# Weights first, batch 0's small loads on another queue: a fused sparse-attention and FFN kernel on one core

## The chip, the cores and the metric

The kernel runs on one core of one Trainium2 chip. The metric is device time in microseconds (us). One core has five engines that run their own instruction streams: TensorE (PE in the profile; its weight loads are PEld), VectorE (DVE), ScalarE (ACT), GpSimd (POOL) and SyncE (SP). Loads and stores are done by 16 DMA engines; SP and ACT issue them, each on a queue of its own (q1 and q10 in the profile).

## The reference

Eight batches of attention with 8 heads, 576 tokens and 64 values a head. Heads 0 to 3 look back over 32 tokens, heads 4 to 7 at the earlier tokens of the same place modulo 32. The 4608 x 512 result goes through a feed-forward layer without activation.

```python
mask_local = (rel >= 0) & (rel < stride)                       # stride = 32
mask_strided = (rel >= 0) & (pos[None, :] % stride == pos[:, None] % stride)
scores = np.where(masks[None], scale * q @ k^T, -1e9)          # local: heads 0-3, strided: heads 4-7
attn = softmax(scores)
x = (attn @ v).transpose(0, 2, 1, 3).reshape(B * S, H * D)     # 4608 x 512
a = x @ w1                                                     # w1, w2: 512 x 1024
b = x @ w2
h = a * b @ w3                                                 # w3: 1024 x 1024
out = h @ w_out                                                # w_out: 1024 x 512
```

Inputs and output are f32 in HBM.

## The kernel before

**The fold.** Since nothing stands between `w3` and `w_out`, the kernel first computes their product `w34` (1024 x 512, f16). For each of 8 row blocks `jc` of `w3`, `fold_tr(jc)` transposes the block on PE (8 transposes, line 357) into PSUM, and DVE and ACT each copy one half to `w3T` (lines 359 and 360). `fold_mm(jc)` gives two halves of 4 matmuls of 512 columns each (line 335): `h0` uses the part of `w3T` that DVE copied, `h1` the part that ACT copied; after `h1` the block of `w34` is cast by DVE or ACT in turn. Every half needs `w_out`, all of it by the end of `fold_mm(0)`. The 23 units of the fold stand in the order h0(0), tr(1), h1(0), h0(1), tr(2), h1(1) and so on.

**Attention** works on pairs of heads; pairs 0 and 1 of a batch are local, 2 and 3 strided. A pair's steps: `ph_T` transposes q and k on PE (line 214), copies by ACT or DVE; `ph_R` does the same for the last 64 tokens (line 230), once a batch; `ph_S` computes scores (line 248), ACT the exponential (line 253), DVE the mask (line 255); `ph_PV` multiplies by v (line 268) and DVE divides by the sum (lines 274, 276); `ph_T2` transposes back (line 284) and ACT copies into `xT` (line 70 or 291). Batch 0 has 21 such steps.

**The feed-forward layer** runs over 9 tiles of 512 tokens: `ab_halves` computes a and b (lines 312, 321; 16 units) and their product on DVE (line 323), `o_halves` the output (line 335, 8 units), which ACT copies and stores (lines 346, 347).

**Order.** PE's instructions are pinned in program order. `host` writes that order out: it runs through the units of the fold or of a tile and puts steps of the attention between them, from the unit after `lead` on, spread evenly over the rest, so that after the last unit the stream has come to a given step. Before the change batch 0's 21 steps are spread over the last 20 of the fold's 23 units (`lead=3`), and 8 steps of batch 1 over the last 7 of the 16 `ab` units of tile 0 (`lead=9`). The other engines' orders are found by a scheduler at build time, from the program order and a model of when data is there. Each engine then works in order.

**Loads.** All loads are issued by SP, in program order, into `stgp`, a ring of 9 staging buffers of 4 KB a partition; a load waits until the cast of the ninth load before it is done. Casts to f16 go mostly to POOL (line 74; `load_w12` gives `w1` to ACT, line 70). Row sizes in HBM, as the loads take them: `w3` 4 KB (`load_w3`, line 141), `w_out` 2 KB (`load_wo`, line 136), q and k 1 KB (`load_qk`, line 159), `w1`, `w2` 1 KB (`load_w12`, line 150), the last 64 tokens of q and k 256 B, 512 rows each (`load_rest`, line 168), v of the local heads 256 B, 4 transfers of 576 rows (`load_vL`, line 179), v of the strided heads 2 KB (`load_vS`, lines 190 and 191). The cast blocks of `w3` have 4 buffers (`w3n`), so the cast of block jc + 4 waits for `fold_tr(jc)`.

Before the change `w3`'s eight blocks are loaded in between batch 0's loads, as the end of the listing shows.

Of the kernel before, what the change touches and what calls it, by code (L numbers as in the profile page):

```python
# [8 lines left out]
FP32 = mybir.dt.float32  # L9
# [10 lines left out]
def kernel(  # L20
# [11 lines left out]
    nc = tc.nc  # L32
    B, H, S, D = q.shape
# [3 lines left out]
    P = 128  # L37
# [10 lines left out]
    LQ, LT = 96, 6  # L48
    SQ, ST = 72, 8
    NM = 512  # L50
# [4 lines left out]
    stgp = ctx.enter_context(tc.tile_pool(name="stgp", bufs=9))  # L55
# [9 lines left out]
    def pe(ins):  # L65
        return tc.keep_in_program_order(ins)

    def copy(eng, out, in_):
        if eng == "a":
            nc.scalar.copy(out=out, in_=in_)  # L70
        elif eng == "v":
            nc.vector.tensor_copy(out=out, in_=in_)  # L72
        else:
            nc.gpsimd.tensor_copy(out=out, in_=in_)  # L74
# [46 lines left out]
    xT = [consts.tile([P, NTOK], FP16, name=f"xT{cc}") for cc in range(4)]  # L121
# [11 lines left out]
    def load_wo(g, eng):  # L133
        src = moe_w_out.rearrange("(c p) n -> p c n", p=P)
        st = stgp.tile([P, 2, DM], FP32, tag="stg")
        nc.sync.dma_start(st, src[:, 2 * g:2 * g + 2, :])
        copy(eng, woh[:, 2 * g:2 * g + 2, :], st)

    def load_w3(jc, eng):
        st = stgp.tile([P, DF], FP32, tag="stg")  # L140
        nc.sync.dma_start(st, moe_w3[bass.ds(jc * P, P), :])
        t = ffn.tile([P, DF], FP16, tag="w3n", bufs=4)
        w3n[jc] = t
        copy(eng, t, st)

    def load_w12(g):
        cs = bass.ds(g * 256, 256)
        for wd, wh, eng in ((moe_w1, w1h, "a"), (moe_w2, w2h, "p")):
            st = stgp.tile([P, KM, 256], FP32, tag="stg")
            nc.sync.dma_start(st, wd.rearrange("(c p) n -> p c n", p=P)[:, :, cs])  # L150
            copy(eng, wh[:, :, cs], st)


    x16 = {}

    def load_qk(b, grp, engs="pp"):
        for nm, ten, eng in (("q", q, engs[0]), ("k", k, engs[1])):
            st = stgp.tile([P, 4, 4, D], FP32, tag="stg")
            nc.sync.dma_start(st.rearrange("p h c d -> p h (c d)"),
                              ten[b, 4 * grp:4 * grp + 4, 0:NM].rearrange("h (p c) d -> p h (c d)", c=4))  # L160
            t = qkp.tile([P, 4, 4, D], FP16, tag=f"{nm}{grp}")
            copy(eng, t, st.rearrange("p h c d -> p c h d"))
            x16[(b, nm, grp)] = t

    def load_rest(b, eng="p"):
        st = stgp.tile([P, H, D], FP32, tag="stg")
        for i, ten in enumerate((q, k)):
            nc.sync.dma_start(st[64 * i:64 * i + 64], ten[b, :, NM:S].rearrange("h p d -> p h d"))
        t = qkp.tile([P, H, D], FP16, tag="r")
        copy(eng, t, st)  # L170
        x16[(b, "r")] = t

    def load_vL(b):
        vt = v16L[b % 2]
        for hp in range(2):
            hs = slice(2 * hp, 2 * hp + 2)
            st = stgp.tile([P, 2, LT, D], FP32, tag="stg")
            for h in range(2):
                nc.sync.dma_start(st[32:P, h], v[b, 2 * hp + h].rearrange("(t p) d -> p t d", p=LQ))
            for pr in (bass.ds(32, 32), bass.ds(64, 64)):  # L180
                nc.gpsimd.tensor_copy(out=vt[pr, hs, :, 0:D], in_=st[pr])  # L181
            nc.vector.tensor_copy(out=vt[0:32, hs, 1:LT, 0:D], in_=vt[96:P, hs, 0:LT - 1, 0:D])

    def load_vS(b):
        vt = v16S[b % 2]
        for hp in range(2):
            st = stgp.tile([SQ, 2, ST, D], FP32, tag="stg")
            sf = st.rearrange("p h c d -> p h (c d)")
            sv = v[b, 4 + 2 * hp:6 + 2 * hp].rearrange("h (p c) d -> p h (c d)", c=ST)
            nc.sync.dma_start(sf[0:64], sv[0:64])  # L190
            nc.sync.dma_start(sf[64:SQ], sv[64:SQ])
            nc.gpsimd.tensor_copy(out=vt[:, 2 * hp:2 * hp + 2, :, 0:D], in_=st)  # L192


# [102 lines left out]
    def ab_halves(tch):  # L297
        tok = bass.ds(tch * NT, NT)
        res = []

        def first():
            abts[tch] = ffn.tile([P, KF, NT], FP16, tag="abt", bufs=4, name=f"abt{tch}")

        for jc in range(KF):
            st = {}

            def a(jc=jc, st=st):
                if jc == 0:
                    first()
                aps = psF.tile([P, NT], FP32, tag="f")  # L310
                for ci in range(KM):
                    pe(nc.tensor.matmul(aps, w1h[:, ci, bass.ds(jc * P, P)], xT[ci][:, tok],  # L312
                                        start=(ci == 0), stop=(ci == KM - 1)))
                asb = ffn.tile([P, NT], FP32, tag="asb")
                nc.scalar.copy(out=asb, in_=aps)  # L315
                st["asb"] = asb

            def bb(jc=jc, st=st):
                bps = psF.tile([P, NT], FP32, tag="f")
                for ci in range(KM):  # L320
                    pe(nc.tensor.matmul(bps, w2h[:, ci, bass.ds(jc * P, P)], xT[ci][:, tok],  # L321
                                        start=(ci == 0), stop=(ci == KM - 1)))
                nc.vector.tensor_mul(abts[tch][:, jc, :], bps, st["asb"])  # L323

            res += [a, bb]
        return res
# [26 lines left out]
    def fold_tr(jc):  # L353
        js = bass.ds(jc * P, P)
        ps = psF.tile([P, 1024], FP16, tag="f", name="trp")
        for kc in range(KF):
            pe(nc.tensor.transpose(ps[:, kc * P:(kc + 1) * P], w3n[jc][:, bass.ds(kc * P, P)], id16))
        pv = ps.rearrange("x (c j) -> x c j", j=P)
        nc.vector.tensor_copy(out=w3T[0][:, :, js], in_=pv[:, 0:4, :])
        nc.scalar.copy(out=w3T[1][:, :, js], in_=pv[:, 4:8, :])  # L360

    def fold_mm(jc):
        js = bass.ds(jc * P, P)

        def done(ps):
            copy("va"[jc % 2], w34[:, jc, :], ps)

        return acc_halves(lambda kc: w3T[kc // 4][:, kc % 4, js], lambda kc: woh[:, kc, :], done)
# [3 lines left out]
    batch_end = {}  # L372
# [4 lines left out]
    for b in range(B):  # L377
# [4 lines left out]
        for i in range(4):  # L382
            p = 4 * b + i
# [14 lines left out]
    pos = [0]  # L398

    def host(units, upto, lead=0):  # L400
        n = len(units) - lead
        p0 = pos[0]
        for i, u in enumerate(units):
            u()
            tgt = p0 + ((upto - p0) * max(i + 1 - lead, 0)) // n
            while pos[0] < tgt:
                stream[pos[0]]()
                pos[0] += 1


    load_w3(0, "p")
    for g in range(4):
        load_wo(g, "p")
    load_w3(1, "p")
    load_qk(0, 0)
    load_rest(0)
    load_w3(2, "p")
    load_vL(0)
    load_w3(3, "p")
    load_qk(0, 1)  # L420
    load_w3(4, "p")
    load_w3(5, "p")
    load_vS(0)
    load_w3(6, "p")
    load_w3(7, "p")
    load_w12(0)
    load_w12(1)
    load_w12(2)
    load_qk(1, 0)
    load_rest(1)  # L430
    load_w12(3)
    load_vL(1)
    load_qk(1, 1)
    load_vS(1)

    fold = []
    fold_tr(0)
    for jc in range(KF):
        h0, h1 = fold_mm(jc)
        fold.append(h0)  # L440
        if jc + 1 < KF:
            fold.append(lambda jc=jc: fold_tr(jc + 1))
        fold.append(h1)
    host(fold, batch_end[0], lead=3)
    load_qk(2, 0)
    load_rest(2)
    load_vL(2)
    host(ab_halves(0), pos[0] + 8, lead=9)
    load_qk(2, 1)
    load_vS(2)  # L450
    host(o_halves(0), batch_end[1])
    for tch in range(1, NTILE):
# [46 lines left out]
```

## Time and profile before

| what | value |
|---|---|
| median of 3 runs | 295.0 us (292.44 to 295.15) |
| profiled execution | span 299.8 us, 6132 instructions |
| PE busy | 268.9 us, 90% of the span |
| DVE busy | 174.6 us, 58% |
| ACT busy | 147.1 us, 49% |
| POOL busy | 102.1 us, 34% |
| bytes moved | 48.64 MB, mean 162 GB/s |

The profiled execution's time is its span; recording it makes it longer than the runs without a profile. Busy shares are averages over the whole span: the first 50 us hold the fold and batch 0, the middle a mix of attention and feed-forward tiles, and from about 200 us on the last tiles have less attention beside them. A group's releaser is what ended the idle time before it, and only the idle time of the engine that bounds a stretch costs anything.

### The profile page before, as it was taken

To read this page: it belongs to the slowest core of one execution; us is meant where nothing else is said; L and a number is where in the kernel's file an instruction comes from. 1 tells how busy PE (TensorE), PEld (TensorE's weight loads), DVE (VectorE), ACT (ScalarE), POOL (GpSimd) and SP (SyncE) were. 2 spreads that over 40 slices of the span, in tenths; PEclk is the share of its full clock that TensorE was granted. 3 is DMA by queue.
4 is the path that set the end of the run, shared out by engine and by line. 5 is a ranking of instruction groups with operands and counts; after the bars stand their busy time and mean duration, and the time that the engine had idled before them with its cause. 6 is when DMAs were issued, how large, how long until landed. Compare 5 with 4: busy or idle time off the path is not lost.

```text
span 299.8 us, 6132 instructions
## 1 busy us (share of the span) xinstructions
PE 268.9 (90%) x2401; PEld 141.6 (47%) x2401; DVE 174.6 (58%) x353; ACT 147.1 (49%) x269; POOL 102.1 (34%) x118
## 2 busy tenths in 40 slices
PE   2258898989889989989999899999999999999995
PEld 1025554435545545545555445555555555444442
DVE  2011775357888866886789659747765774340430
ACT  2025586557565545536645554564455445333332
POOL 5539744486626724653455345110000000000000
PEclk9996999999999999999999999999999999999999
DMA  7999999999869929994896796030012002003003
GB/s 228 349 160 352 288 348 258 216 273 209 249 200 243 242 79 270 246 178 159 240 236 140 253 193 164 27 115 2 2 57 87 0 2 105 35 2 116 24 2 140
DMA packets 58653, 48.64 MB, mean 162 GB/s; under 512 B 29184, under 2 KB 49664, under 8 KB 58624
## 3 DMA queue, kind: packets, MB, share of 16 engines
q1 hardware_dynamic: 53440, 38.81, 54.7%
q10 hardware_dynamic: 5184, 9.44, 8.7%
q8 instruction: 19, 0.31, 0.5%
q14 instruction: 10, 0.08, 0.1%
HBM read 38.80 MB, written 9.44 MB: 161 GB/s over the span
## 4 chain that ended last, share of the span: by engine, by line
PE 67%; DVE 9%; DMA 9%; ACT 9%; issue 3%; SPq 1%; POOL 0%; ACTq 0%
PE ops L335 19%; PE bps L321 18%; PE aps L312 16%; PE xps L268 4%; PE ps L214 4%; DMA st<-in_moe_w_dram 4%; ACT pte L253 3%; DVE ptm L255 3%; DMA st<-in_moe_w_out_dram 3%; DMA out_dram<-osb 3%; PE sps L248 2%; PE ps L284 2%; DVE abt L323 2%; ACT xT L291 2%; DVE kT L72 2%
## 5 line engine op out<-in xcount | busy, mean ns | idle before, releaser
L312 PE MATMUL aps<-xT,w1h 128*128 128x512 f16 x288 | 75.3, 379 | 3.2 <-ACT xT L291 3.0
L323 DVE TENSOR_TENSOR abt<-bps,asb 128x512 f16<-128x512 f32 x72 | 49.5, 687 | 47.2 <-PE bps L321 45.5
L321 PE MATMUL bps<-xT,w2h 128*128 128x512 f16 x288 | 74.0, 379 | 0.0
L315 ACT COPY asb<-aps 128x512 f32<-128x512 f32 x72 | 42.2, 586 | 64.6 <-PE aps L312 61.8
L335 PE MATMUL ops<-w,abt 128*128 128x512 f16 x288 | 71.7, 379 | 0.5 <-DVE abt L323 0.5
L74 POOL CAST t<-st 128x1024 f16<-128x1024 f32 (+1 forms) x48 | 47.4, 991 | 43.4 <-DMA st<-in_k_dram 29.1
L253 ACT ACTIVATE pte<-sps 128x576 f16<-128x576 f32 (+1 forms) x64 | 38.4, 650 | 7.3 <-PE sps L248 7.1
L276 DVE TENSOR_TENSOR xqs<-xps,rcp 96x384 f16<-96x384 f32 (+1 forms) x64 | 39.6, 619 | 2.0
L321 PEld LDWEIGHTS <-w2h 128*128 128x128 f16 x288 | 25.8, 97 | 31.6 <-issue 5.1
L70 ACT COPY qT<-ps 128x512 f16<-128x512 f16 (+1 forms) x48 | 22.9, 481 | 29.9 <-PE ps L214 23.8
L346 ACT COPY osb<-ops 128x512 f32<-128x512 f32 x36 | 21.1, 586 | 29.9 <-PE ops L335 28.6
L335 PEld LDWEIGHTS <-abt 128*128 128x128 f16 x288 | 24.7, 98 | 23.1 <-DVE abt L323 1.0
L312 PEld LDWEIGHTS <-w1h 128*128 128x128 f16 x288 | 25.1, 98 | 22.2
L181 POOL CAST v16L<-st 32x768 f16<-32x768 f32 (+1 forms) x32 | 27.1, 847 | 18.4 <-DMA st<-in_v_dram 12.6
L268 PEld LDWEIGHTS <-ptm 72*128 72x128 f16 (+1 forms) x448 | 21.4, 97 | 19.2 <-DVE ptm L255 6.4
L255 DVE TENSOR_TENSOR ptm<-pte,maskL 128x576 f16<-128x576 f16 x32 | 20.5, 646 | 11.7 <-ACT pte L253 11.2
L72 DVE COPY kT<-ps 128x512 f16<-128x512 f16 (+1 forms) x36 | 18.8, 535 | 10.1 <-ACT qT L70 10.0
L255 DVE TENSOR_TENSOR ptm<-pte,maskS 72x576 f16<-72x576 f16 x32 | 19.6, 620 | 8.5 <-ACT pte L253 7.9
L192 POOL CAST v16S<-st 72x1024 f16<-72x1024 f32 x16 | 16.9, 1055 | 20.1 <-PE xps L268 11.4
L335 PE MATMUL ops<-woh,w3T 128*128 128x512 f16 x64 | 19.8, 440 | 3.2 <-POOL woh L74 3.1
L214 PEld LDWEIGHTS <-t 128*128 128x128 f16 x256 | 17.1, 99 | 8.8 <-issue 2.6
L214 PE MATMUL ps<-id,t 128*128 128x128 f16 x256 | 20.1, 222 | 0.5 <-POOL t L74 0.5
(48 smaller groups left out, 175.8 us busy)
## 6 DMA issues: line engine op xcount, KB each, us to landing
out_dram<-osb ACTq DMA_DIRECT2D x36, 256.0 KB, 2.0
st<-in_moe_w_dram SPq DMA_DIRECT2D x16, 512.0 KB, 8.9
st<-in_q_dram SPq DMA_DIRECT2D x16, 512.0 KB, 5.5
st<-in_k_dram SPq DMA_DIRECT2D x16, 512.0 KB, 6.6
st<-in_v_dram SPq DMA_DIRECT2D x32, 144.0 KB, 6.1
st<-in_v_dram SPq DMA_DIRECT2D x16, 256.0 KB, 7.2
st<-in_moe_w_out_dram SPq DMA_DIRECT2D x4, 512.0 KB, 8.5
st<-in_q_dram SPq DMA_DIRECT2D x8, 128.0 KB, 8.1
```

The source lines that it names most:

```text
L74: nc.gpsimd.tensor_copy(out=out, in_=in_)
L181: nc.gpsimd.tensor_copy(out=vt[pr, hs, :, 0:D], in_=st[pr])
L214: pe(nc.tensor.transpose(ps[:, i, c * P:(c + 1) * P], src[:, c, h0:h0 + 2].rearrange("p h d -> p (h d)"), id16))
L253: nc.scalar.activation(out=pte[0:kr], in_=sps[0:kr, :, 0:288], func=AF.Exp, bias=0.0, scale=scale)
L255: nc.vector.tensor_mul(ptm[0:kr, 0:576].rearrange("p (a x) -> p a x", x=w), pte[0:kr].rearrange("p h (a x) -> p (h a) x", x=w), _ap(mk, 0, ...
L268: pe(nc.tensor.matmul(xps[:, h, i * 65:(i + 1) * 65], ptm[0:kr, c0:c0 + P], vt[0:kr, 2 * (s.hp % 2) + h, g * m + i, :], start=True, stop=T ...
L276: nc.vector.tensor_mul(xqs[0:w, 0:m].rearrange("p i h d -> p h i d"), xv[:, :, :, 0:D], _ap(rcp, 0, [[rp, w], [4, 2], [1, m], [0, D]]))
L312: pe(nc.tensor.matmul(aps, w1h[:, ci, bass.ds(jc * P, P)], xT[ci][:, tok], start=(ci == 0), stop=(ci == KM - 1)))
L315: nc.scalar.copy(out=asb, in_=aps)
L321: pe(nc.tensor.matmul(bps, w2h[:, ci, bass.ds(jc * P, P)], xT[ci][:, tok], start=(ci == 0), stop=(ci == KM - 1)))
L323: nc.vector.tensor_mul(abts[tch][:, jc, :], bps, st["asb"])
L335: pe(nc.tensor.matmul(st["ps"], lhs(ci), rhs(ci), start=(ci == 0), stop=(ci == KF - 1)))
```

## The change

SP now issues `w3(0)`, the four parts of `w_out` and `w3(1)` to `w3(4)` one after the other, then q and k of heads 0 to 3, `w3(5)`, q and k of heads 4 to 7, `w3(6)`, `w3(7)`. Batch 0's `load_rest`, `load_vL` and `load_vS` go to ACT's queue: ten transfers, issued behind ACT's copy of `fold_tr(0)` and pinned there. They don't use the staging ring but columns of `xT` that are written only from batch 2 on. Seven of the casts of `w3` and `w_out` move from POOL to DVE. Batch 0's 21 steps are spread over the last 8 of the fold's 23 units (`lead=15`), and in tile 0 the steps of batch 1 begin two units later (`lead=11`).

```diff
+    def spare(cc, n):
+        return xT[cc][:, 2 * S:2 * S + 2 * n].bitcast(FP32)
+
+    def act_dma(out, in_):
+        pe(nc.scalar.dma_start(out, in_))
...
-    def load_rest(b, eng="p"):
-        st = stgp.tile([P, H, D], FP32, tag="stg")
+    def load_rest(b, early=False):
+        if early:
+            st = spare(3, H * D).rearrange("p (h d) -> p h d", h=H)
+        else:
+            st = stgp.tile([P, H, D], FP32, tag="stg")
+        dma = act_dma if early else nc.sync.dma_start
         for i, ten in enumerate((q, k)):
-            nc.sync.dma_start(st[64 * i:64 * i + 64], ...)
+            dma(st[64 * i:64 * i + 64], ...)
...
-    def load_vL(b):
+    def load_vL(b, early=False):
...
+            if early:
+                st = spare(0, 4 * LT * D).rearrange("p (h t d) -> p h t d", h=4, t=LT)[:, hs]
+            else:
+                st = stgp.tile([P, 2, LT, D], FP32, tag="stg")
+            dma = act_dma if early else nc.sync.dma_start
...
-    def load_vS(b):
+    def load_vS(b, early=False):
...
+            if early:
+                st = spare(1 + hp, 2 * ST * D)[0:SQ].rearrange("p (h c d) -> p h c d", h=2, c=ST)
+            else:
+                st = stgp.tile([SQ, 2, ST, D], FP32, tag="stg")
+            dma = act_dma if early else nc.sync.dma_start
...
-    load_w3(0, "p")
+    load_w3(0, "v")
     for g in range(4):
-        load_wo(g, "p")
-    load_w3(1, "p")
+        load_wo(g, "pv"[g % 2])
+    for jc in range(1, 5):
+        load_w3(jc, "pv"[jc % 2])
     load_qk(0, 0)
-    load_rest(0)
-    load_w3(2, "p")
-    load_vL(0)
-    load_w3(3, "p")
+    load_w3(5, "v")
     load_qk(0, 1)
-    load_w3(4, "p")
-    load_w3(5, "p")
-    load_vS(0)
     load_w3(6, "p")
-    load_w3(7, "p")
+    load_w3(7, "v")
     load_w12(0)
...
     fold_tr(0)
+    load_rest(0, early=True)
+    load_vL(0, early=True)
+    load_vS(0, early=True)
...
-    host(fold, batch_end[0], lead=3)
+    host(fold, batch_end[0], lead=15)
...
-    host(ab_halves(0), pos[0] + 8, lead=9)
+    host(ab_halves(0), pos[0] + 8, lead=11)
```

More of the change, by code (lines that the diff above doesn't have):

```diff
@@ L163, in load_qk @@
             x16[(b, nm, grp)] = t
-    def load_rest(b, eng="p"):
-        st = stgp.tile([P, H, D], FP32, tag="stg")
+    def load_rest(b, early=False):
[4 more added lines that the diff above has]
+        dma = act_dma if early else nc.sync.dma_start
         for i, ten in enumerate((q, k)):
-            nc.sync.dma_start(st[64 * i:64 * i + 64], ten[b, :, NM:S].rearrange("h p d -> p h d"))
+            dma(st[64 * i:64 * i + 64], ten[b, :, NM:S].rearrange("h p d -> p h d"))
         t = qkp.tile([P, H, D], FP16, tag="r")
-        copy(eng, t, st)
+        copy("p", t, st)
         x16[(b, "r")] = t
-    def load_vL(b):
+    def load_vL(b, early=False):
         vt = v16L[b % 2]
@@ L176, in load_vL @@
             hs = slice(2 * hp, 2 * hp + 2)
-            st = stgp.tile([P, 2, LT, D], FP32, tag="stg")
+            if early:
[3 more added lines that the diff above has]
+            dma = act_dma if early else nc.sync.dma_start
             for h in range(2):
-                nc.sync.dma_start(st[32:P, h], v[b, 2 * hp + h].rearrange("(t p) d -> p t d", p=LQ))
+                dma(st[32:P, h], v[b, 2 * hp + h].rearrange("(t p) d -> p t d", p=LQ))
             for pr in (bass.ds(32, 32), bass.ds(64, 64)):
@@ L182, in load_vL @@
             nc.vector.tensor_copy(out=vt[0:32, hs, 1:LT, 0:D], in_=vt[96:P, hs, 0:LT - 1, 0:D])
-    def load_vS(b):
+    def load_vS(b, early=False):
         vt = v16S[b % 2]
         for hp in range(2):
-            st = stgp.tile([SQ, 2, ST, D], FP32, tag="stg")
+            if early:
[3 more added lines that the diff above has]
+            dma = act_dma if early else nc.sync.dma_start
             sf = st.rearrange("p h c d -> p h (c d)")
             sv = v[b, 4 + 2 * hp:6 + 2 * hp].rearrange("h (p c) d -> p h (c d)", c=ST)
-            nc.sync.dma_start(sf[0:64], sv[0:64])
-            nc.sync.dma_start(sf[64:SQ], sv[64:SQ])
+            dma(sf[0:64], sv[0:64])
+            dma(sf[64:SQ], sv[64:SQ])
             nc.gpsimd.tensor_copy(out=vt[:, 2 * hp:2 * hp + 2, :, 0:D], in_=st)
```

## The prediction

> **What bounds the kernel now.** I read the page's strip of 40 slices first, then busy time by stretches, the chain of waits, SyncE's (SP's) and the matrix engine's rows in order of time, and last the DMA view of single stretches.
>
> The page's strip (7.5 us a digit):
>
> ```profile
> PE   2258898989889989989999899999999999999995
> PEclk9996999999999999999999999999999999999999
> DMA  7999999999869929994896796030012002003003
> ```
>
> TensorE (PE) is full from slice 4 to the end; its holes are the first three slices, and the granted clock is low in the fourth. There the DMA engines are full. So the kernel is bound by loads up to about 24 us and by PE after that. The same as busy time by stretches (stretch, its length, busy us of PE, weight load, VectorE (DVE), ScalarE (ACT), GpSimd (POOL), clock, DMA share, GB/s):
>
> ```profile
> 7.60:14.60 7.00, 1.32 (x4) 0.13 (x3) 0.00 (x0) 0.00 (x0) 4.16 (x4) 1.00 1.07 360
> 14.60:23.40 8.80, 4.54 (x24) 2.35 (x24) 1.12 (x2) 1.66 (x3) 3.73 (x4) 0.88 1.15 165
> 23.40:30.00 6.60, 6.17 (x48) 3.85 (x48) 1.41 (x4) 3.94 (x10) 6.27 (x7) 0.64 1.03 373
> 30.00:50.10 20.10, 17.95 (x224) 11.06 (x225) 14.47 (x32) 15.14 (x26) 11.21 (x11) 1.00 1.10 307
> ```
>
> From 14.6 to 23.4 us the loads move 165 GB/s instead of 360: the 256-byte rows of `load_rest` and `load_vL`. After the idle time the clock is 0.64 for 6.6 us, which costs PE 6.17 x 0.36 = 2.2 us. The chain of waits (start, length, what):
>
> ```profile
> 2.75 8.86 DMA st<-in_moe_w_out_dram
> 11.61 10.69 DMA st<-in_moe_w_dram
> 22.36 1.05 POOL t L74
> 23.45 1.03 PE trp L357 x8
> ```
>
> w3(2) ends the wait at 22.3 us. What is to be won is the 4.3 us that PE idles in the second stretch, some of the 5.7 us in the first, and the 2.2 us of clock.
>
> **What the loads allow.** Everything the fold and batch 0 need is 9.83 MB (w3 4.19, w_out 2.10, q and k 2.10, rest 0.26, v 1.18), and the DMA view of 2.6 to 36.5 us shows 9.84 MB. The change moves the same bytes in the same row sizes. So the last of them lands near 36 us after it too, whatever the order, unless two queues together move more than one. That decides whether the change can gain: what lands last must be what is needed last.
>
> **What a load on ACT's queue waits for.** In the trace only the stores use that queue. The one issued at 72.34 us, in the two stretches after it:
>
> ```profile
> q1 hardware_dynamic: 1220, 0.90, 110.1%
> ...
> q1 hardware_dynamic: 463, 0.63, 81.8%
> q10 hardware_dynamic: 136, 0.25, 25.6%
> ```
>
> Until 75.7 us 1220 packets of SP's queue (q1) go by and none of the store's (q10); then the 136 pass together with SP's later ones. Over all 36 stores the landing takes 2.0 us in the median and 6.5 at most. So ACT's transfers are served in order of issue, behind what SP had issued before. The Trainium skill, page "DMA: Bandwidth & Descriptors", section "Queues, rings and completion order", says instead that each DMA engine takes turns between the queues packet by packet. By the store's row the small loads wait their full turn; by that rule they would pass at once beside SP's large ones, which is the faster rival below.
>
> The second limit is in the issuing itself (start, length):
>
> ```profile
> 6.13 5.36 SPq L168 DMA_DIRECT2D st<-in_k_dram  x1
> 11.61 2.04 SPq L141 DMA_DIRECT2D st<-in_moe_w_dram  x1
> 13.74 5.41 SPq L179 DMA_DIRECT2D st<-in_v_dram  x4
> ```
>
> An issue of `load_rest` takes 0.60 us when nothing is in its way (median later), the four of `load_vL` 2.2. Here one takes 5.36 and four 5.41. When the first let go at 11.5 us, SP had issued 3328 rows (128 + 4x256 + 128 + 4x512), and the DMA view of 0 to 11.5 us holds 1511 packets, 91 of them under 512 B (completions): 1420 rows started, some 1,900 left. I take 1,900 outstanding rows as the point from which an issue holds its engine. On SP that cost little. **On ACT it holds everything behind it.**
>
> **The change, part by part.**
>
> *w3(1) to w3(4) next to w_out.* Nine staging buffers let SP issue these nine loads without waiting, so w3(2) to w3(4) land 1.35 us apart behind w3(1), cast by 16 to 19 us instead of 23.4 to 34. That removes the chain's 10.69 us DMA piece. q and k of heads 0 to 3 come 4 us later (3 x 1.35); batch 0 now starts late, so that is free.
>
> *Casts to DVE.* Seven of 128x1024 f32. No such row is in the trace: bounds 0.42 us (the f16 128x512 copy, L359) and 1.4 us (twice the 0.69 us of the 128x512 cast from PSUM, L72); I take 1.0, near POOL's 1.04. DVE is busy 1.12 us of the 8.8 before 23.4, so all seven are hidden: 0 us. Without that cover 3 us (w3(5), w3(7) and one more ahead of batch 0's masks). One risk goes with them: DVE works in order, and a cast of w3(7) that waits for its load holds the masks behind it.
>
> *Ten loads on ACT's queue.* They stand behind the copy of `fold_tr(0)`, at 6.9 us. By then SP has issued some 5.8 MB, of which 1.4 are served; at 360 GB/s the rest takes 12 us, so ACT's first row is served at about 19 us. ACT's ten loads are 1024 + 2304 + 288 = 3616 rows. If the limit counts each queue by itself, the last issue waits until 3616 - 1900 = 1716 are served: at about 500 rows a us (1034 packets from 19 to 21 us) 3.4 us more, so ACT is free at 22.5 us. If both queues share it, ACT and SP take the room in turns: 3616 rows of ACT's and about as many of SP's must be served first, near 30 us. Service in one common order speaks for a common store, the rows for neither; I take the middle, 26 us, and keep both ends. Below that, 13 us, if it never holds (10 issues at 0.6).
>
> Queued behind it on ACT: the second half of `fold_tr(1)`'s copy (L360). PE can do `h0(0)`, `tr1`, `h1(0)`, `h0(1)`, `tr2` and then stops, at about 16.5 us, until ACT is free. So the 10.69 us wait for w3(2) turns into a wait for ACT of up to 9.5 us, at the same place, and the low clock comes with it again (2 us).
>
> *Batch 0 later (lead 15).* Of its 15 units ahead, 7 halves and 3 transposes then remain, 7x0.86 + 3x0.45 = 7.4 us, with the low clock some 10: batch 0 starts at 26 + 10 = 36 us, with 8 fold units (6x0.86 + 2x0.45 = 6.1 us of PE) and its own 8.5 us (4x0.45 of L214, 0.4 of L230, 4x0.45 of L248, 8x0.36 of L268, 4x0.42 of L284). That is 14.6 us of PE, and on ACT 8 exponentials x 0.65, 8 copies x 0.59, 4 x 0.28, 4 x 0.66 and 6 of the fold and w1 of 0.6 to 1.05: 17 to 19 us. In the stretch to 50.1 us ACT was busy 15.14 of 20.1. Squeezed into fewer fold units, ACT is the bound: 17.5 us. Batch 0 then ends at 53.5 us instead of 50.1: **+3.5 us.**
>
> If ACT is not held at all, it comes to the same by another road: then all ten loads are in line ahead of w3(6) and w3(7), which land last, near 36 us; `fold_tr(6)` stands in PE's order ahead of 19 of batch 0's 21 steps, and 37.5 + 15.5 is 53.
>
> *lead 9 to 11 in tile 0.* Two units of 0.86 us earlier, three steps of batch 1 later. The w1 cast (0.75 us at 58.0 us in the chain) then lies off the path, as its load lands near 57 in both: -0.2 to -0.75 us; I take -0.2.
>
> *Behind that* PE is 90 to 96% busy, and the shift passes through.
>
> **Sum:** +3.5 - 0.2 = +3.3 us on the profiled span of 299.8, 303.1. That span is 4.8 us above the median of the runs, 295.0; carried over one for one, **298.3 us**.
>
> **The rivals.**
>
> *No change: each queue has its own limit.* ACT is free at 22.5 us, batch 0 starts at 32.5 and ends at 50 to 50.5. +0.2: 295. For it: SP's rows alone explain the 1,900. Against: the common order of service.
>
> *Much slower: one limit for both, ACT held to 30 us.* Batch 0 starts at 39.5 and ends at 57: +7 us, 302. For it: the store's row. Against: stores later take 0.34 us to issue with 1,500 rows of SP's outstanding, so nothing shows ACT held yet.
>
> *Faster: the small rows pass beside the large ones.* If the queues take turns, ACT needs 1716 rows at some 140 a us (one each beside SP's 2 to 4 KB rows): free at 19 us. w3(6) and w3(7) land near 29, batch 0 starts at 29.5, ends at 46 to 47: -3.5 us, 291.5. It decides from ACT free before about 22 us with w3(6) there by 30. For it: a stretch where stores and 256-byte rows ran together moved 245 GB/s (114 to 116 us) against 165. Against: the store at 72.34 us. The rule of the Trainium skill's page "DMA: Bandwidth & Descriptors", section "Queues, rings and completion order", would give this time; the store's row does not agree with it.
>
> **How the numbers follow.** Slower by about 3 us: 0.40. No change: 0.20. Much slower: 0.12. Faster: 0.28. The range goes from somewhat beyond the faster case, 289.5 (its landing 2 us better), to just above the much slower one, 303; under 2 in 10 lies outside. A measurement of this kernel (292.4 to 295.2 in three runs) tells about 1%, 3 us, from nothing. Faster by over 1% is most of the faster case: 0.27. Within 1%: no change, and the milder part of the forecast: 0.27. Slower: 0.46. Alone, the forecast's own range is 296 to 301.
>
> **What would show it.** Right: ACT's ten issues last from 7 us to past 22; its next copy (L360) waits for them; PE idles from about 16 to past 22 with a clock near 0.6 after it; the store rule holds (ACT's rows served after q and k of heads 0 to 3); the first L312 starts after 52 us. Wrong: ten issues of 0.6 us each and w3(7) cast by 31 us; batch 0's last `xT` copy before 49; or a total load time for the 9.83 MB well under 34 us.

## The result and the profile after

| what | before | after |
|---|---|---|
| median of the runs | 295.07 us (292.44 to 296.62, 4 runs) | 325.47 us (321.64 to 329.14, 4 runs) |
| ratio, 95% interval | | 1.099 (1.089 to 1.109) |
| profiled execution's span | 299.8 us | 322.8 us |
| PE busy | 268.9 us | 273.3 us |

The change costs 30 us. The forecast was 3 us, with 303.0 as the upper end of the range. The ratio leaves out the run of 329.14 us, which lies more than 1.5% above the fastest of its kernel, so it is a little below the quotient of the medians.

The two spans differ by 23.0 us, the medians by 30.4. In every run on record the time lies 1.7 to 1.9 us above the span. So the span of 299.8 us belongs to a time of some 301.6 us (an estimate), longer than any timed run of the kernel before (291.21 to 299.79). Recording is not what lengthened it: the profiled execution of the kernel after is one of its four timed runs, 324.64 us with a span of 322.8. A comparison of the two traces shows some 7 us less than the medians do.

The strip of 40 slices of the kernel after (8.1 us a digit) shows where: PE's holes now reach to slice 9, and the low clock comes twice.

```profile
PE   1625263678978899999999999999999999999994
PEclk9985695699999999999999999999999999999999
DMA  7999999999961799399674551002002001102003
```

The same as busy time by stretches, with the columns and the cuts of before (stretch, length, PE, weight load, DVE, ACT, POOL, clock, DMA share, GB/s):

```profile
14.60:23.40 8.80, 3.49 (x15) 1.67 (x13) 1.72 (x3) 0.00 (x0) 2.39 (x2) 0.88 1.20 244
23.40:30.00 6.60, 2.08 (x5) 0.73 (x6) 1.34 (x3) 1.22 (x3) 4.50 (x5) 0.50 1.13 235
30.00:50.10 20.10, 10.18 (x60) 5.27 (x58) 3.66 (x6) 6.55 (x10) 9.44 (x10) 0.75 1.09 313
50.10:62.00 11.90, 7.06 (x58) 4.90 (x59) 4.33 (x9) 5.62 (x13) 7.66 (x9) 0.50 1.03 240
```

In the first stretch ACT does nothing at all. From 30 to 50.1 us PE is busy 10.2 us where it was 17.95. The loads are not slower on the whole: 244 GB/s in the first stretch instead of 165, 235 instead of 373 in the second, and from 2.6 to 36.5 us 10.22 MB instead of 9.84. PE's rows in order of time say what it waits for. The bracket is the idle time before the row and what ended it:

```profile
27.93 3.59 PE L353 MATMUL ops<-woh,w3T 128*128 128x512 f16 x8 [9.84 <-ACT w3T L378]
38.65 1.89 PE L353 MATMUL ops<-woh,w3T 128*128 128x512 f16 x4 [5.78 <-DVE w3T L377]
52.90 0.61 PE L248 MATMUL ps<-id,t 128*128 128x128 f16 x4 [6.94 <-POOL t L74]
```

Three waits on three engines: 9.84 + 5.78 + 6.94 = 22.6 us. They partly replace the old wait for w3(2), so the sum is no proof; the experiments take the waits one by one. (Lines have moved: L353 is L335 of before, L375 L357, L377 and L378 L359 and L360, L248 L230, L232 L214, L330 L312.)

**The wait on ACT.** ACT's rows in order of time; ACTq rows are its DMA issues, and a row with x8 reaches from the first to the last of eight:

```profile
9.40 0.73 ACTq L160 DMA_DIRECT2D xT<-in_q_dram  x1
10.17 0.71 ACTq L160 DMA_DIRECT2D xT<-in_k_dram  x1
10.92 16.33 ACTq L160 DMA_DIRECT2D xT<-in_v_dram  x8
27.29 1.07 ACT L378 COPY w3T<-trp 128x512 f16<-128x512 f16 x2 [17.31 <-DVE v16L L196]
```

The ten issues last from 9.40 to 27.24 us, 17.8 us in all, and the copy that PE needs stands behind them. Asked for single issues, the same view shows that they are not one long hold:

```profile
12.16 1.69 ACTq L160 DMA_DIRECT2D xT<-in_v_dram  x1
...
16.42 3.52 ACTq L160 DMA_DIRECT2D xT<-in_v_dram  x1
19.98 1.64 ACTq L160 DMA_DIRECT2D xT<-in_v_dram  x1
23.44 0.51 ACTq L160 DMA_DIRECT2D xT<-in_v_dram  x1
...
26.96 0.28 ACTq L160 DMA_DIRECT2D xT<-in_v_dram  x1
```

The ten take 11.8 us. Between them lie five gaps of 0.3 to 2.1 us, 5.9 us together, and each ends 0.02 to 0.03 us after some load has landed. The chain of waits has one:

```profile
3.27 8.88 DMA st<-in_moe_w_dram
12.14 0.02 issue
12.16 11.26 DMA xT<-in_v_dram
```

w3(1) lands at 12.14, and the second v load is issued at 12.16, though it needs nothing of w3(1). The built program says why, in its own list of what each instruction waits for:

```
ACT  xT<-in_q_dram   [waits DMAHW0]     ACT  xT<-in_v_dram   [waits DMAHW5]
ACT  xT<-in_k_dram   [waits DMAHW2]     ACT  xT<-in_v_dram   [waits DMAHW7]
ACT  xT<-in_v_dram   [waits DMAHW4]     ACT  xT<-in_v_dram   [waits DMAHW1]   ...
SP   st<-in_moe_w_dram (w3(5))  [waits DMAHW0, Pool]
```

All loads and stores of the program, on both queues, share eight completion semaphores (DMAHW0 to 7; a semaphore is a counter on which an engine can wait). A load waits, in the engine that issues it, until the load before it on its semaphore has landed. By the trace's landing records the five late issues wait for w3(1), w3(3) and then for ACT's own second, third and fourth v load (23.42, 24.22 and 26.94 us). It works the other way too: SP's w3(5) waits 4.5 us for ACT's load of q's rest.

**The wait on DVE.** DVE's rows:

```profile
37.07 1.20 DVE L72 CAST t<-st 128x1024 f16<-128x1024 f32 x1 [7.86 <-DMA st<-in_moe_w_dram]
38.19 0.41 DVE L377 COPY w3T<-trp 128x512 f16<-128x512 f16 x1
```

The cast of w3(7) waits for a load that SP issued only at 26.21 us; the copy that PE needs stands behind it. That issue is late by the semaphores too: w3(7) follows w3(5) on DMAHW0, w3(5) was itself issued only at 18.40 us, behind the landing of q's rest (18.34), and landed at 26.15. (The chain of waits names POOL ahead of 26.21, but POOL's semaphore had reached the value that this issue needs at 14.54 us.)

**The wait on POOL.** POOL's rows; the cast of batch 0's rest reads `xT`, that of batch 1 reads `st`:

```profile
51.67 0.62 POOL L74 CAST t<-st 128x512 f16<-128x512 f32 x1 [0.71 <-DMA st<-in_k_dram]
52.23 0.62 POOL L74 CAST t<-xT 128x512 f16<-128x512 f32 x1
```

Batch 0's rest had landed at 21.0 us. Its cast follows that of batch 1, because `load_rest(0)` now stands behind `load_rest(1)` in the program, and the two buffers of tag "r" are handed out in program order.

### The profile page after: what moved, and what is told of

Read it like the earlier page. It is cut to its first block, busy times and chain, and to the rows that moved or that the text cites. A ratio compares the mean times of both kernels' runs of the same rounds, so it can differ in the third digit from the quotient of the medians.

```text
span 322.8 us, 6137 instructions
## 1 busy us (share of the span) xinstructions
PE 273.3 (85%) x2401; PEld 144.7 (45%) x2401; DVE 170.7 (53%) x360; ACT 147.2 (46%) x269; POOL 94.1 (29%) x111
## 4 chain that ended last, share of the span: by engine, by line
PE 71%; DMA 12%; ACT 8%; DVE 4%; issue 2%; POOL 1%; SPq 1%; ACTq 0%; POOLq 0%; DVEq 0%
PE ops L353 20%; PE bps L339 20%; PE aps L330 18%; DMA st<-in_moe_w_dram 9%; PE ps L232 4%; PE xps L286 4%; DMA xT<-in_v_dram 3%; PE sps L266 3%; ACT pte L271 3%; PE ps L302 2%; DVE ptm L273 2%; ACT xT L309 1%; DVE xqs L294 1%; ACT osb L364 1%; ACT kT L70 1%
## 5 line engine op out<-in xcount | busy, mean ns | idle before, releaser
L330 PE MATMUL aps<-xT,w1h 128*128 128x512 f16 x288 | 75.3, 379 | 1.8 <-ACT xT L309 1.5
L353 PE MATMUL ops<-w,abt 128*128 128x512 f16 x288 | 71.5, 379 | 0.0
L74 POOL CAST t<-st 128x1024 f16<-128x1024 f32 (+1 forms) x42 | 41.1, 992 | 37.3 <-DMA st<-in_q_dram 12.0
L353 PE MATMUL ops<-woh,w3T 128*128 128x512 f16 x64 | 22.6, 503 | 19.1 <-ACT w3T L378 9.8
L330 PEld LDWEIGHTS <-w1h 128*128 128x128 f16 x288 | 25.2, 98 | 22.5
L195 POOL CAST v16L<-st 32x768 f16<-32x768 f32 (+1 forms) x28 | 23.6, 843 | 39.4 <-PE xps L286 21.4
L353 PEld LDWEIGHTS <-abt 128*128 128x128 f16 x288 | 24.7, 98 | 22.2
L286 PEld LDWEIGHTS <-ptm 72*128 72x128 f16 (+1 forms) x448 | 21.6, 98 | 20.3 <-DVE ptm L273 7.8
L210 POOL CAST v16S<-st 72x1024 f16<-72x1024 f32 x14 | 14.9, 1061 | 30.0 <-PE xps L286 29.4
L273 DVE TENSOR_TENSOR ptm<-pte,maskS 72x576 f16<-72x576 f16 x32 | 18.0, 564 | 10.3 <-ACT pte L271 9.6
L273 DVE TENSOR_TENSOR ptm<-pte,maskL 128x576 f16<-128x576 f16 x32 | 16.9, 535 | 11.9 <-ACT pte L271 11.4
L232 PE MATMUL ps<-id,t 128*128 128x128 f16 x256 | 20.3, 225 | 1.3 <-ACT kT L70 1.3
L232 PEld LDWEIGHTS <-t 128*128 128x128 f16 x256 | 17.2, 101 | 8.3 <-issue 3.1
```

The source lines that it names most:

```text
L232: pe(nc.tensor.transpose(ps[:, i, c * P:(c + 1) * P], src[:, c, h0:h0 + 2].rearrange("p h d -> p (h d)"), id16))
L273: nc.vector.tensor_mul(ptm[0:kr, 0:576].rearrange("p (a x) -> p a x", x=w), pte[0:kr].rearrange("p h (a x) -> p (h a) x", x=w), _ap(mk, 0, ...
L286: pe(nc.tensor.matmul(xps[:, h, i * 65:(i + 1) * 65], ptm[0:kr, c0:c0 + P], vt[0:kr, 2 * (s.hp % 2) + h, g * m + i, :], start=True, stop=T ...
L353: pe(nc.tensor.matmul(st["ps"], lhs(ci), rhs(ci), start=(ci == 0), stop=(ci == KF - 1)))
```

## The experiments

All were timed in turns with the kernel before, whose median was 295.1 to 296.2 us in the four groups of runs. "Ratio" is to it, with its 95% interval. Line numbers are those of each run's own kernel.

### One part after the other taken back

**e1**, an own buffer for batch 0's rest:

```diff
-        t = qkp.tile([P, H, D], FP16, tag="r")
+        t = qkp.tile([P, H, D], FP16, tag="r0" if early else "r", bufs=1 if early else 2, name="rt")
```

> The changed kernel with batch 0's f16 tile of the last 64 tokens in a buffer of its own instead of the ring of two that it shares with batch 1's, so that its cast stands ahead of batch 1's on POOL. Theory 'three waits in a row' (ACT held by its ten issues 9.8 us, DVE behind the cast of w3(7) 5.8 us, POOL's cast of batch 0's rest behind batch 1's 6.9 us): the third wait goes, 316 us (-9, with some of the low clock). Rival 'squeezed batch 0' (lead 15 costs it): no change, 325 us. Rival 'loads too late' (q, k and v land later than before): no change, 325 us.

Measured: 318.36 us, ratio 1.080 (1.070 to 1.091). PE's wait for POOL is gone, what is left ahead of L248 is 1.16 us for ACT. That wait was worth 7.1 us (325.47 to 318.36).

**e2**, the ten loads on SP's queue, behind q and k of heads 0 to 3 (their program order ends the wait for POOL too):

```diff
-        pe(nc.scalar.dma_start(out, in_))
+        nc.sync.dma_start(out, in_)
...
     load_qk(0, 0)
+    load_rest(0, early=True)
+    load_vL(0, early=True)
+    load_vS(0, early=True)
```

> The changed kernel with batch 0's ten small loads issued by SP instead of ACT, right behind q and k of heads 0 to 3, into the same places; the cast of batch 0's rest is then traced ahead of batch 1's. Theory 'three waits in a row': ACT's hold and POOL's wait go, the wait of DVE for w3(7) stays: 307 us. Rival 'squeezed batch 0': 322 to 325 us. Rival 'loads too late': 325 us or more, since w3(5) to w3(7) now land behind all of batch 0's small loads.

Measured: 309.49 us, ratio 1.053 (1.044 to 1.062). ACT's hold was worth 8.9 us beside e1, as far as the new order on SP costs nothing of its own. PE still waits 6.9 us at L375, for a cast on DVE.

**e3**, e1 with the casts of w3(5) and w3(7) back on POOL:

```diff
-    load_w3(5, "v")
+    load_w3(5, "p")
...
-    load_w3(7, "v")
+    load_w3(7, "p")
```

> As the first, and the casts of w3(5) and w3(7) on POOL instead of DVE. Theory 'three waits in a row': the second wait goes too, 311 us; ACT's hold stays. Rival 'squeezed batch 0': 325 us. Rival 'loads too late': 325 us.

Measured: 319.57 us, ratio 1.075 (1.060 to 1.089): nothing that can be told from e1, a miss. PE now waits 4.64 us for ACT, where a cast of w1 stands ahead of the copy for `w3T` and waits for its own late load. ACT's rows:

```profile
39.60 1.05 ACT L70 CAST w1h<-st 128x1024 f16<-128x1024 f32 x1 [7.49 <-DMA st<-in_moe_w_dram]
40.55 0.58 ACT L378 COPY w3T<-trp 128x512 f16<-128x512 f16 x1
```

The cast of w1 stood ahead of that copy already (at 38.49 us in the kernel after, 37.48 in e1), and the wait for DVE hid it. Whose cast is in front does not matter when SP's loads are late.

**e4** and **e8**, the kernel before with the new leads, both and the fold's alone:

```diff
-    host(fold, batch_end[0], lead=3)
+    host(fold, batch_end[0], lead=15)
...
-    host(ab_halves(0), pos[0] + 8, lead=9)
+    host(ab_halves(0), pos[0] + 8, lead=11)
```

> The kernel before with the two leads alone (15 and 11). Theory 'three waits in a row': the leads cost little by themselves, 297 to 300 us, from PE waiting for w3(6) with two steps of batch 0 done. Rival 'squeezed batch 0': most of the 30 us, 315 us or more. Rival 'loads too late': no change, 295 us.

> The kernel before with lead 15 in the fold and lead 9 left in tile 0. Theory 'the squeezed batch 0 costs it': its 21 steps between 8 fold units are bound by the chain PE, ScalarE, VectorE, PE of each pair, 304 to 307 like both leads together (306.6). Rival 'the later batch 1 in tile 0 costs half': 300 to 302.

Measured: e4 306.56 us, ratio 1.044 (1.032 to 1.056); e8 306.93 us, ratio 1.038 (1.033 to 1.044). The squeezed batch 0 costs 11 us by itself and lead 11 nothing that can be told. e4's time lies between the 297 to 300 us of the first theory and the 315 of its rival. PE's rows of e8:

```profile
27.20 0.62 PE L357 MATMUL trp<-id,t 128*128 128x128 f16 x8 [1.88 <-POOL t L74]
30.92 0.62 PE L357 MATMUL trp<-id,t 128*128 128x128 f16 x8 [1.37 <-POOL t L74]
33.93 0.62 PE L357 MATMUL trp<-id,t 128*128 128x128 f16 x8 [0.67 <-POOL t L74]
37.89 0.38 PE L230 MATMUL ps<-id,t 128*128 128x128 f16 x4 [1.16 <-ACT kT L70]
42.89 0.51 PE L268 MATMUL xps<-v16L,ptm 128*128 128x65 f16 x6 [2.79 <-ACT pte L253]
50.03 0.35 PE L268 MATMUL xps<-v16L,ptm 128*128 128x65 f16 x6 [1.10 <-DVE ptm L255]
52.28 0.30 PE L248 MATMUL sps<-qT,kT 64*128 64x72 f16 x8 [0.33 <-DVE xqs L276]
```

Two losses. While the fold waits for w3 blocks (the rows of L357), PE has no step of batch 0 to put in between. And then the steps of a pair wait for each other over PE, ACT and DVE, with too few fold units in between: from L230 at 37.89 to the first L312 at 60.62 are 22.7 us, in the kernel after 22.7 as well (52.90 to 75.61). No engine is full in them: of 22.7 us PE is busy 15.5 in e8 and 16.3 in the kernel after, ACT 16.2 and 13.4, DVE 11.8 and 13.9. The low clock is no likely bound either: the length is the same with a clock of 0.72 and then 1.00 in e8 as with 0.50 and then 0.99 in the kernel after.

**e5**, e1 with the leads of before (3 and 9):

> The kernel after with an own buffer for batch 0's rest and the leads of before (3 and 9). Theory 'the costs add': 325.5 - 7 (own buffer) - 11 (leads) = 307, with ScalarE still held to about 27 us and PE still waiting some 9 us at the copy of line 378. Rival 'the late start decides': batch 0 cannot start before ScalarE is free at 27 us, so it is squeezed whatever the lead; then the leads are worth little here, 315 to 318. A third: all that is left is the hold, and with the early w3 it is even: 300 or less.

Measured: 310.72 us, ratio 1.047 (1.040 to 1.055). The squeeze is worth 7.6 us here. ACT is still held to 27.8 us.

**e6**, the kernel before with only the ten loads on ACT's queue (own rest buffer):

> The kernel before, with only batch 0's ten small loads moved to ScalarE's queue (own rest buffer, no squeeze, casts and order of w3 as before). Theory 'an issue holds ScalarE while the rows ahead are outstanding': ScalarE cannot copy for w3T from about 9 to 25 us, PE waits there until about 26 instead of 22.3 for w3(2): 4 to 6 us slower, 300 to 302. Rival 'the hold costs only together with the early w3 blocks': w3(2) and w3(3) land sooner because the small rows are no longer ahead of them, 293 to 296. Rival 'the hold costs its whole length': 16 us, 310.

Measured: 312.31 us, ratio 1.059 (1.053 to 1.065), the rival "its whole length". ACT's row of the eight v loads:

```profile
11.25 20.89 ACTq L160 DMA_DIRECT2D xT<-in_v_dram  x8
```

And the row of PE that waits for ACT:

```profile
33.80 0.59 PE L248 MATMUL ps<-id,rt 128*128 128x128 f16 x4 [13.06 <-ACT kT L70]
```

Of the 20.9 us, the eight issues themselves take 3.5; the rest are waits for landings.

**e7**, e2 with the leads of before. What is left of the change is the early w3 and the shared casts:

> The kernel after with the ten loads issued by SyncE behind q and k of heads 0 to 3, and the leads of before: what is left of the change is the early w3 and the shared casts. Theory 'the costs add': 309.5 - 11 = 298.5. Rival 'the early w3 gains the idle time of 14.6 to 23.4 us': 291 to 293. Rival 'with w3(5) to w3(7) late the fold waits for them whatever the lead': 305.

Measured: 298.12 us, ratio 1.011 (1.005 to 1.017).

So the 30 us come apart along one path: own buffer -7.1 (325.47 to 318.36), leads -7.6 (to 310.72), queue -12.6 (to 298.12), early w3 and casts -2.3 (to 295.82). The shares depend on the order: with the queue taken back first (e1 to e2 to e7) it is worth 8.9 and the leads 11.4.

### What holds ACT

Three kernels made from e5. **e9** takes batch 0's rest and local v as the same bytes in 512 rows instead of 3328; they are other tokens, so it leaves out the right result for batch 0. **e10** leaves the rows and takes issues away, and **e13** turns e10's order round.

```diff
 e9
-            dma(st[64 * i:64 * i + 64], ten[b, :, NM:S].rearrange("h p d -> p h d"))
+                dma(st[64 * i:64 * i + 64].rearrange("p h d -> p (h d)"),
+                    ten[b, 0, 0:NM].rearrange("(p c) d -> p (c d)", p=64))
...
-                dma(st[32:P, h], v[b, 2 * hp + h].rearrange("(t p) d -> p t d", p=LQ))
+                    dma(st[32:P, h].rearrange("p t d -> p (t d)"),
+                        v[b, 2 * hp + h].rearrange("(p t) d -> p (t d)", p=LQ))
 e10, e13: one issue for four heads; load_vS(0) on SP
+            if early and hp == 0:
+                dma(spare(0, 4 * LT * D)[32:P].rearrange("p (g d) -> p g d", d=D),
+                    v[b, 0:4].rearrange("h (t p) d -> p (h t) d", p=LQ))
```

> The kernel e5 (after, own rest buffer, leads 3 and 9) in which batch 0's rest and local v come as the same bytes in 512 rows of 1.5 and 2 KB instead of 3328 of 256 B; they are other tokens, so batch 0's output is not the reference's. Ten issues on ScalarE as before. Theory 'rows' (prediction): 800 rows in all never reach 1,900, so the ten issues take 0.3 to 0.7 us each and ScalarE is free at about 16 us. Theory 'completion semaphores' (each load waits until the load eight before it has landed): the issues still start at landings, the last waits for the own v loads, so ScalarE is free at 19 to 22 us. Either way the DMA engines save some 8 us of small rows: 293 to 300 us against 310.7.

> The kernel e5 with the four loads of local v merged into one issue of the same 2304 rows, and the four loads of strided v (288 rows) back on SyncE: ScalarE issues 3328 of its 3616 rows, but in three issues, none of which waits for a load that was not issued by 3 us. Theory 'rows': ScalarE is held about as long as in e5, to 25 us or later. Theory 'completion semaphores': what is left is the issue of 2304 rows itself, 1.5 to 7 us from 11 us on, ScalarE free at 13 to 19 us; with SyncE's loads no longer woven with ScalarE's, 299 to 304 us against 310.7.

> The kernel e10 with its three issues on ScalarE turned round: the 2304 rows of local v first, then the 1024 rows of the rest in two issues. Theory 'semaphores alone': the two issues behind it start at the landings they wait for, w_out's last part at about 11 and w3(2) at about 13.5 us, and take 0.6 us each, ScalarE free at 14 us. Theory 'rows also hold': the issue behind the 2304 rows lasts until most of them are served (some 200 rows a us beside SyncE's), ScalarE free at 18 us or later, and its share of the 17.8 us in the kernel after is that of the long issues, 11.8 us. In time 303 to 308 in the first case (e10: 306.4), 308 to 313 in the second.

Measured, e9: 301.80 us, ratio 1.018 (1.009 to 1.028), just above the 293 to 300 expected; ACT's rows:

```profile
10.30 12.16 ACTq L160 DMA_DIRECT2D xT<-in_v_dram  x8
22.50 0.59 ACT L386 COPY w3T<-trp 128x512 f16<-128x512 f16 x1 [12.87 <-DVE v16L L204]
```

With 800 rows no issue takes more than 0.66 us, and ACT is still held to 22.46: of 13.4 us, 8.3 are five gaps that end at landings. Here the semaphores alone hold it.

e10: 306.40 us, ratio 1.034 (1.026 to 1.041). ACT issues 92% of the rows in 2.1 us and goes on:

```profile
10.68 0.61 ACTq L160 DMA_DIRECT2D xT<-in_v_dram  x1
14.24 0.59 ACT L381 COPY w3T<-trp 128x512 f16<-128x512 f16 x1 [4.47 <-DVE w3T L380]
```

But the time is above the 299 to 304 us expected, since the 2304 rows land only at 31.0 us, 20.3 after their issue, and an SP load on the same semaphore waits for them with every later load behind it. SP's rows:

```profile
20.21 0.61 SPq L211 DMA_DIRECT2D xT<-in_v_dram  x1
31.02 0.29 SPq L212 DMA_DIRECT2D xT<-in_v_dram  x1
```

e13: 304.25 us, ratio 1.035 (1.026 to 1.044). The rows hold as well, but only an issue behind them; ACT is free at 19.6 us:

```profile
9.21 0.39 ACTq L160 DMA_DIRECT2D xT<-in_v_dram  x1
10.87 5.79 ACTq L160 DMA_DIRECT2D xT<-in_q_dram  x1
16.70 2.94 ACTq L160 DMA_DIRECT2D xT<-in_k_dram  x1
```

The 2304 rows are handed over in 0.39 us, the next 512 take 5.79. So both theories hold a part. Of the 17.8 us of the kernel after, 5.9 are waits for semaphores and 11.8 are issues; ten issues without rows in their way take 4.9 (e9), so some 7 of these are put down to rows. The expected time for that case, 308 to 313, was a miss: the hold is shorter than e5's and ends before the data of batch 0 is there.

**Order of service.** e10's queues from 14 to 18 us, in the DMA view (packets, MB, share of the DMA engines):

```profile
q1 hardware_dynamic: 858, 0.99, 83.8%
q10 hardware_dynamic: 865, 0.22, 26.8%
```

They take turns; in five stretches of e10 from 14 to 27 us the two counts differ by 7 at most. The kernel after does it from 14 to 16 us (396 and 394 packets), but not from 16 to 18:

```profile
q10 hardware_dynamic: 953, 0.24, 89.5%
q1 hardware_dynamic: 189, 0.18, 37.9%
```

SP's load of k, issued at 13.51 us, was still outstanding there; it landed at 22.81. Why its rows came so late stays open. Nor is the start served in turns: the first row of the issue at 9.40 us is served at 13.60, and until then 443 of the 529 rows go by that SP had issued and that had not begun. The Trainium skill's rule (page "DMA: Bandwidth & Descriptors", section "Queues, rings and completion order") that a DMA engine takes turns between the queues agrees with e10's counts. It gives neither the wait at the start nor the kernel after's counts from 16 to 18 us.

### A form without the hold

**e11** and **e12**: all loads on SP in nearly the order of before, first casts shared with DVE, leads 3 and 9:

```diff
 e11
+    load_w3(2, "p")
     load_qk(0, 0)
     load_rest(0, early=True)
-    load_w3(2, "p")
+    load_w3(3, "p")
     load_vL(0, early=True)
-    load_w3(3, "p")
     load_qk(0, 1)
 e12: w3(3) ahead of load_qk(0, 0) too, load_vS(0) ahead of w3(5)
```

> A candidate: all loads on SyncE in the order of before, but w3(2) ahead of q and k of heads 0 to 3 and w3(3) ahead of local v, the first casts shared with VectorE, batch 0's small loads in columns of xT, leads 3 and 9. Theory 'only w3(2) behind the 256-byte rows makes the idle time of 14.6 to 23.4 us': 291 to 293 (before 295.8). Rival 'the loads are moved about within the same 36 us': 295 to 297, as e7 (298.1).

> The same with w3(2) and w3(3) both ahead of q and k, and q and k of heads 4 to 7 ahead of w3(4). If it is the w3 blocks that PE lacks early: 290 to 292, ahead of e11. If batch 0's late data costs as in e7: 296 to 298, behind e11.

Measured: e11 296.20 us, ratio 0.999 (0.993 to 1.004); e12 297.22 us, ratio 1.009 (1.004 to 1.014). The idle time at 14.6 us is gone in e11 (PE busy 7.12 of 8.8 us), and comes back as 4.52 of 6.6 us in the next stretch. Both came out as their rivals said, 295 to 297 and 296 to 298 us. The loads are only moved about within the same time.

**e14** and **e15**: e10's three issues as ACT's first instructions, and that with e11's order on SP:

```diff
+    load_rest(0, early=True)
+    load_vL(0, early=True)
     load_w3(0, "v")
     for g in range(4):
```

> The three issues of e10 as ScalarE's first instructions, before any weights, with e10's order on SyncE. No issue waits for a semaphore and none stands ahead of a copy. If the hold is all that the queue costs: 294 to 299. The price: the 3328 small rows take turns with w3(0) and w_out, the fold starts 2 to 4 us later than at 9 us. If the casts on GpSimd that now stand ahead of w3(2)'s wait for v: 300 to 304.

> e14 with SyncE's order of e11 (w3(2), q and k of heads 0 to 3, w3(3), q and k of heads 4 to 7, then the rest of w3). If e14 loses by late q and k as e7 did: 2 to 4 us better than e14, 292 to 296, and the only form here that could beat the kernel before. If the late start of the fold decides: as e14.

Measured: e14 305.31 us, ratio 1.039 (1.028 to 1.049); e15 303.35 us, ratio 1.032 (1.024 to 1.040). e14 lies just above the 300 to 304 us of its worse case; e15 is 2 us better than e14, but not at the 292 to 296 us that its first theory gave. ACT issues all three in 2.1 us and is not held. The chain of e14 shows what is:

```profile
2.29 17.84 DMA xT<-in_v_dram
22.01 0.99 POOL v16L L198
23.95 4.60 POOL t L74 x4
```

POOL's casts of v stand ahead of casts of w3, q and k and wait 7.9 us for v, whose rows take turns with the weights'. The start of `h0(0)` moves to 11.4 us from 9.2 in e10, as expected. No form tried here beat the kernel before.

## Why the prediction was wrong, point by point

The step that failed is "Batch 0 later": batch 0 was to start at 36 us and to take 17.5 us, bounded by ACT. It started at 45.35 us, waited 6.9 us for POOL, and took 24.2 us besides, in which no engine was full: 9.3 + 6.9 + 6.7 us too much.

**What the loads allow: right.** The last of what the fold and batch 0 need, w3(7), lands at 36.9 us (26.21 + 10.73 in the chain), for "near 36 us".

**"ACT's transfers are served in order of issue": wrong as a rule for all rows.** In e10 the queues take turns for 13 us; in the kernel after they do so in one stretch and not in the next. The store's row at 72.34 us had shown only the wait at the start, behind rows that were already outstanding. The rival drawn from the rejected rule, 291.5 us, did not come either: its conditions were ACT free before about 22 us and w3(6) there by 30. In e10 ACT was free at 14.2 us, but SP could issue w3(6) only at 31.4.

**What holds ACT: right place, half the mechanism.** 26 us were taken, 27.24 measured; PE's wait at that copy is 9.84 us, "up to 9.5" was said. That is partly luck: 26 was the middle of two bounds, 22.5 and 30, that both knew only outstanding rows. The waits of an issue for an earlier load's landing, 5.9 us here and nearly all of the hold in e6, were in neither.

**w3(1) to w3(4) early: right, and worth nothing.** They had landed by 16.38 us; the wait behind them became ACT's, and without that wait (e7, 298.12 us) the time is no better than before.

**"Casts to DVE: 0 us": the risk named was the price.** Six of the seven casts take 0.69 us, where 1.0 was taken. "A cast of w3(7) that waits for its load holds the masks behind it" was priced at nothing; it held a copy for `w3T` and PE for 5.78 us. e3 shows that this is no price of DVE: moved to POOL, the same lateness of SP's loads came out on ACT. By the landings that hold back w3(5) and w3(7), it is the second price of the shared semaphores.

**Own rest: not seen.** 7.1 us (e1). The step that moved `load_rest(0)` behind the loads of batch 1 counted its issues and not its cast, which moved with it on POOL's queue. A moved call has to be followed on every engine that it uses.

**Batch 0 "starts at 36": 9 us too early.** Its first transposes (L232) start at 45.35 us: 1.2 us from ACT, 0.7 until PE's next matmul, 5.8 from w3(7), and the fold part took 11.6 instead of 10.

**"Squeezed batch 0 takes 17.5 us bounded by ACT": 6 to 7 us too small.** It takes 24.2 us from its first transposes to the end of its last copy into `xT` (76.45 us), POOL's wait taken off. The part from L248 to the first L330, 22.7 us, is the same in e8 without any hold. The sum counted ACT's busy time. But no engine is full there (ACT 13.4 of 22.7 us); the rows show PE waiting for ACT and DVE in turn, the way PE, ACT, DVE, PE within a pair. Measured by itself the lead costs 11 us, where 3.5 were forecast for it and ACT's hold together.

Added up on the end of batch 0, its last copy into `xT` (50.1 us in before's trace), forecast at 53.5 and measured at 76.45 us: 1.2 + 0.7 + 5.8 + 1.6 + 6.9 (POOL) + 6.7 (24.2 us instead of 17.5) = 22.9 of 23.0.

**lead 11: too small to tell** (-0.2 forecast; e4 and e8 can't be told apart). **Behind it the shift passes through: nearly**, 23.0 us at that point are 19.7 at the end (322.8 against 303.1).

**From the span to the median: 7.5 us more.** The sum took off 4.8 us, as before's span lies that far above its median. The kernel after's median, 325.47 us, lies 2.7 above its span instead. Before's trace is of a long execution: from the first L312 to its end it takes 250.6 us, where the kernel after's takes 247.2 and those of the experiments 245.1 to 250.4. So 19.7 + 7.5 = 27.2 us are what separates 298.3 from 325.47.

Of the signs, "ACT's ten issues from 7 to past 22", "its next copy waits for them", "PE idles from about 16 to past 22 with a clock near 0.6" (18.1 to 27.9 us, 0.50) and "the first L312 after 52" came true. "The store rule holds" did not.

## What to carry to other kernels

A DMA issued from an engine that also computes is a wait in that engine's order: ask which load each issue must see landed first (here the one before it on one of eight shared semaphores), and what stands behind it. When a call is moved in the program, follow its cast and its buffer as well as its transfers. And a chain of short steps over three engines, squeezed into fewer units of other work, is bound by the way round and not by the busiest engine, so its price is read from the idle time between its steps.

## What the runs showed of the hardware

- A load of 2304 rows is handed over in 0.39 to 0.64 us; the next issue on the same queue then takes 5.79 us for 512 rows (e13). No single number of outstanding rows fits all issues, so what exactly sets that length stays open.
- Two queues served in turns move 301 GB/s of mixed 256-byte and larger rows (e10, 14 to 18 us), against 165 in the stretch of before (14.6 to 23.4 us) in which 2949 of 3171 packets were under 512 bytes. It gained nothing here, since the 2304 rows then took 20.3 us to land.
